# Folding the weights' halves before a merge, and ordering the transform's features by parity

## The chip, the cores and the metric

The kernel runs on one core of a Trainium2 chip. The metric is device time in microseconds (us) of one execution, the median of several runs. A core has TensorE (PE in the profile, its weight loads PEld), VectorE (DVE), ScalarE (ACT), GpSimd (POOL) and SyncE (SP, which issues most transfers). Each works through its own list in order and waits for the others by semaphores. SBUF is the working memory of 128 partitions, PSUM the eight banks into which TensorE adds.

## The reference

The input x has 8 batches of 3008 rows and 256 features. The reference takes a Fourier transform over the rows and one over the features, keeps the real part, and feeds the result to a gated layer:

```python
X = np.fft.fft(np.fft.fft(x, axis=1), axis=2).real
gate = 1.0 / (1.0 + np.exp(-(X @ w_gate)))      # w_gate, w_val: 256 x 1536
out = (gate * (X @ w_val)) @ w_out              # w_out: 1536 x 256
```

All is float32 in the result; the weights arrive as float64 and are turned to float32 on the chip.

## The kernel before

The transform over the rows is done with cosine and sine tables, on sums and differences of mirrored rows and features ("folds" of x). It leaves, per batch, two tiles of 128 features by 1505 frequencies: pk (cosine) and qk (sine). The transform over the 256 features is never done on the data. It is multiplied into the weights once: dt holds a 256 x 256 table (128 partitions, two halves t, 256 columns: 128 cosine and 128 sine), and a *merge* (`merge`, lines 410 to 421) multiplies it with a piece of 256 columns of w_gate or w_val. Out come pieces of G1 (for pk) and G2 (for qk). There are twelve such pieces, six for each of the two weights.

A piece goes through a chain on all engines. `weight_load` issues its transfer; `weight_parts` (ScalarE, lines 382 and 383) and `weight_join` (VectorE, lines 392 to 395, then GpSimd, line 397) turn float64 into float32; `weight_use` merges it: for each of two column halves h and each row half t of the weights one matmul, that is four calls in float32, and two copies by ScalarE (lines 417, 418) take the bank to G2 and G1. Two small transfers then put one row of G2 into ge. Float32 matmuls appear in the profile as two passes per call, so a merge counts 8 passes.

The order of work is written out by hand; there is no scheduler. After the start (lines 950 to 1015: the first two pieces, and batch 0's row transform) one loop runs over i, 576 times: 8 batches, 6 chunks of up to 252 frequencies, 12 blocks of 128 hidden columns. Per i, `front_a` and `front_b` multiply G1 with pk and G2 with qk into a bank (pf), `gate_a` and `gate_b` apply the gate on ScalarE and VectorE, with sums of blocks (sf) on GpSimd, and `back` multiplies with the output weights (po). Lists such as `use`, `join`, `pre`, `side`, `gap` and `mid` say at which i each further operation is put in; pieces 2 to 13 of the weights are merged at i = 0 to 8, alongside the first iterations.

Batch 0's row transform is done by `half` (line 595): banks ev and od, 24 matmul calls of 377 or 376 columns, from x folded by `half_rows` on VectorE. Batches 1 to 7 use `quarter` (line 620), twice per batch, put in by `mid`: 48 calls, each with 32 (or 31) partitions of x as weights and 95 columns of a table, four partition groups (TILES) writing four banks (sum). `e_sums` does a single feature (the 129th) with one or seven weight columns, placed in four column groups (pe).

In the first stage the order on VectorE is: joins of pieces 0 and 1, then the folds of x in four slices, then the join of piece 2 and the combining of ev and od into pk and qk. ScalarE has the copies of merges 0 and 1. On TensorE four calls named warm on dt come first, then merges 0 and 1, then pe, ev and od slice by slice.

Of the kernel before, what the change touches and what calls it, by code (L numbers as in the profile page):

```python
# [81 lines left out]
def kernel(  # L82
# [49 lines left out]
    def mm(o, l, r, start, stop):  # L132
        nc.tensor.matmul(o, l, r, start=start, stop=stop, skip_group_check=True)  # L133

    def bank(name, other=None):
        if other is not None:
            return pso.tile([P, 512], F32, name=name, tag=f"po{other}")
        return psx.tile([P, 512], F32, name=name, tag="x")
# [41 lines left out]
    wf = const.tile([P, NG, len(PLACE), P], F32, name="wf")  # L180
    G1 = const.tile([P, 2, F], F32, name="G1")
    G2 = const.tile([P, 2, F], F32, name="G2")
    ge = const.tile([P, 2, NFT], F32, name="ge")
# [99 lines left out]
    def quarter_ops():  # L283
# [28 lines left out]
        def ends_r():  # L312
# [10 lines left out]
            (0, 5), (1, 5), (2, 2), (2, 3), (2, 4), (2, 5)]  # L323
    RAW, WS = {}, {}
    shared = {}
    KEEP = 10

    def weight_load(j):
# [32 lines left out]
        else:  # L361
# [6 lines left out]
        raw = raw.bitcast(I32).rearrange("p (c f w) -> p c f w", c=2, w=2)  # L368
        ws = ws.rearrange("p (c f) -> p c f", c=2)
        WS[j] = ws  # L370
        if src.dtype == F32:
            nc.sync.dma_start(out=ws, in_=src)
        else:
            RAW[j] = raw
            nc.sync.dma_start(out=raw.rearrange("p c f w -> p c (f w)"), in_=src.bitcast(I32))  # L375
# [9 lines left out]
    def weight_join(j):  # L385
        if j not in RAW:
            return
        raw, ws = RAW.pop(j), WS[j]
        lo, hi = raw[:, :, :, 0], raw[:, :, :, 1]
        wi = ws.bitcast(I32)  # L390
        ts = nc.vector.tensor_scalar
        ts(out=ws, in0=ws, scalar1=2.0 ** -15, scalar2=HUGE, op0=ALU.max, op1=ALU.min)
        ts(out=wi, in0=wi, scalar1=3, scalar2=0x3FFFFFF8, op0=ALU.logical_shift_left,
           op1=ALU.bitwise_and)
        nc.vector.scalar_tensor_tensor(out=wi, in0=hi, scalar=-(2 ** 30), in1=wi,
                                       op0=ALU.bitwise_and, op1=ALU.bitwise_or)
        nc.gpsimd.tensor_tensor(wi, wi, lo, op=ALU.add)
# [5 lines left out]
    def weight_use(j):  # L403
# [3 lines left out]
        else:  # L407
            merge(WS.pop(j), w, c, (4, 2, 3)[next(turns) % 3] if j > 1 else None)

    def merge(ws, g, c, other):  # L410
        cs = slice(c * WC, (c + 1) * WC)
        ps = bank("ps", other)
        for h in range(2):
            for t in range(2):
                mm(ps[:, h * WC : (h + 1) * WC], dt[:, t, h * HD : (h + 1) * HD], ws[:, t, :],
                   h == 0 and t == 0, t == 1)
        nc.scalar.copy(G2[:, g, cs], ps[:, WC : 2 * WC])
        nc.scalar.copy(G1[:, g, cs], ps[:, 0:WC])
        for f in range(c * WC // P, (c + 1) * WC // P):
            nc.sync.dma_start(  # L420
                out=ge[:, g, f : f + 1], in_=G2[0:1, g, f * P : (f + 1) * P])

# [171 lines left out]

    def half(b, w, d, blk, sn, other=None):

# [23 lines left out]
    def quarter(b, blk):  # L620

        ps = [bank("sum", t + 1) for t in range(4)]
        for what in range(2):
            for part in range(2):
                for q in range(N3):
                    for t, (g, par, lo) in enumerate(TILES):
# [5 lines left out]
                        else:  # L632
                            w, tab = q + N3 * what, TAB["e4"][rows, what ^ g, q]
                        c0 = (2 * what + 1 - part) * NQ4
                        mm(ps[t][:, c0 : c0 + NQ4], W[b, blk][what][rows, w], tab,
                           what == part == q == 0, q == N3 - 1)
        for t, (g, par, lo) in enumerate(TILES):
# [335 lines left out]
    e0 = shared["qk"][:, 4 * WC : 4 * WC + CH]  # L973
    nc.gpsimd.memset(e0, 0.0)
    weight_parts(0)
    weight_parts(1)
# [26 lines left out]
    for f in places_c:  # L1003
        f()
    nc.scalar.copy(e0[0:1], E0[0][:, 0:CH])
    weight_parts(3)
# [239 lines left out]
```

## Time and profile before

| | |
|---|---|
| Median of 3 runs | 1908.67 us (1908.12 to 1909.44) |
| The profiled execution | 1909.15 us, of it span 1907.4 us |
| TensorE busy | 1895.6 us, 99% of the span, 11836 passes |
| VectorE, GpSimd, ScalarE busy | 1520.6, 1543.4, 1353.2 us |
| TensorE clock granted | 1.00 |
| Merges (ps) in the main loop | 10, each 8 passes, 1.73 us on the chain |
| Sum blocks (sum) | 14, each 96 passes, 2.86 us on the chain |

In the groups of the profile, a line such as "L133 PE MATMUL sum<-st,x x1344" names the line of the kernel, the engine, the operation, the tile written and those read, and the number of passes, then the least, median and greatest duration in ns. L133 is the line of the helper `mm`, so matmuls are told apart by their tiles. The duration of a matmul holds its way through the array; the distance of two starts says what one costs in a stream. In the timeline, brackets hold the idle time before an instruction and what ended it.

### The profile page before, as it was taken

Reading aid. Unit: us, or ns where it says so; the run is one execution under the profiler, and the core shown is the slowest. Engines: PE = TensorE matmul, PEld = TensorE weight load, DVE = VectorE, ACT = ScalarE, POOL = GpSimd, SP = SyncE. Lnnn points to the kernel's source line nnn. Section 1 sums busy time; section 2 is a strip of 40 time slices with the busy share of each in tenths; the row PEclk is TensorE's granted clock in tenths of the full one; section 3 lists DMA queues with packets and bytes.
Section 4 is the critical chain, followed back from the end, with each engine's and each line's share of the span. In section 5 each row is a group of like instructions: output and inputs, shape, how many; then the busy total and the mean of one; then the engine's idle time right before and its main releaser. Section 6 shows DMA issues by size and latency. Waiting matters only on the chain.

```text
span 1907.4 us, 36057 instructions
## 1 busy us (share of the span) xinstructions
PE 1895.6 (99%) x11836; PEld 1756.6 (92%) x11836; DVE 1520.6 (80%) x3375; ACT 1353.2 (71%) x3235; POOL 1543.4 (81%) x2733
## 2 busy tenths in 40 slices
PE   8999999999999999999999999999999999999999
PEld 5788999999999999999999999999999999999998
DVE  7678888878979778897788878888788777977775
ACT  4777777777777777777777777677767777777775
POOL 2489879987999779997799878999789986877770
PEclk9999999999999999999999999999999999999999
DMA  8446221212022121211211212122120110010001
GB/s 315 120 134 80 71 89 51 72 33 81 21 64 54 31 87 32 62 41 37 89 39 48 45 39 81 40 52 58 30 74 17 36 37 15 15 25 17 15 18 30
DMA packets 197333, 109.33 MB, mean 57 GB/s; under 512 B 134823, under 2 KB 188818, under 8 KB 195354
## 3 DMA queue, kind: packets, MB, share of 16 engines
q1 hardware_dynamic: 196568, 106.50, 21.1%
q8 instruction: 95, 1.56, 0.3%
q14 instruction: 92, 0.75, 0.1%
q10 hardware_dynamic: 546, 0.51, 0.1%
q0 software_dynamic: 32, 0.00, 0.0%
HBM read 71.24 MB, written 47.87 MB: 62 GB/s over the span
## 4 chain that ended last, share of the span: by engine, by line
PE 94%; DMA 2%; SPq 1%; POOL 1%; ACT 1%; DVE 0%; issue 0%; ACTq 0%; POOLq 0%
PE pf L133 49%; PE po L133 41%; PE sum L133 2%; DMA rtab<-in_stab_dram 1%; PE ps L133 1%; POOL sf L824 1%; DMA st<-in_stab_dram 1%; SPq L206 1%; DMA raw<-in_moe_w_val_dram 0%; PE od L133 0%; POOL x L507 0%; SPq L192 0%; SPq L375 0%; PE pe L133 0%; PE ev L133 0%
## 5 line engine op out<-in xcount | busy, mean ns | idle before, releaser
L824 POOL TENSOR_TENSOR sf<-h,sf 128x168 f32<-128x168 f32 (+1 forms) x1104 | 621.0, 582 | 79.5 <-DVE h L818 75.9
L824 POOL TENSOR_TENSOR sf<-h 128x168 f32<-128x168 f32 (+1 forms) x920 | 519.3, 584 | 159.8 <-DVE h L818 158.0
L133 PE MATMUL pf<-qk,G 128*128 128x252 f32 (+1 forms) x2304 | 583.4, 376 | 0.9 <-ACT ae L787 0.8
L133 PE MATMUL pf<-pk,G 128*128 128x252 f32 (+1 forms) x2304 | 582.7, 376 | 0.0
L772 ACT ACTIVATE pf<-ek,ge 128x252 f32<-128x252 f32 (+1 forms) x1142 | 538.2, 471 | 23.2 <-DMA ge<-G 3.0
L133 PE MATMUL po<-sf,wf 128*128 128x168 f32 (+1 forms) x2944 | 508.3, 305 | 0.0
L787 ACT ACTIVATE ae<-pf 128x504 f32<-128x504 f32 (+1 forms) x576 | 338.8, 588 | 218.7 <-PE pf L133 217.2
L133 PEld LDWEIGHTS pf<-pk,G 128*128 128x128 f32 x2304 | 435.9, 190 | 53.3 <-ACT pf L772 1.5
L133 PE MATMUL po<-h,wf 128*128 128x168 f32 (+2 forms) x2584 | 461.3, 307 | 0.0
L133 PEld LDWEIGHTS po<-sf,wf 128*128 128x128 f32 x2944 | 453.4, 190 | 8.0
L818 DVE TENSOR_TENSOR h<-pf,z 128x252 f32<-128x252 f32 (+1 forms) x576 | 240.4, 417 | 274.0 <-ACT pf L815 270.5
L802 DVE TENSOR_TENSOR z<-ae,pf 128x504 f32<-128x504 f32 (+1 forms) x576 | 384.6, 668 | 83.1 <-ACT h L801 79.1
L908 DVE TENSOR_TENSOR c<-c 128x168 f32<-128x168 f32 (+1 forms) x920 | 438.7, 500 | 3.3
L133 PEld LDWEIGHTS pf<-qk,G 128*128 128x128 f32 x2304 | 410.6, 190 | 32.3 <-ACT ae L787 2.1
L133 PEld LDWEIGHTS po<-h,wf 128*128 128x128 f32 x2584 | 410.4, 190 | 17.8 <-issue 0.9
L801 ACT ACTIVATE h<-pf 128x252 f32<-128x252 f32 (+1 forms) x576 | 216.9, 376 | 146.3 <-PE pf L133 129.0
L815 ACT ACTIVATE pf<-z 128x252 f32<-128x252 f32 (+1 forms) x576 | 214.3, 372 | 116.4 <-DVE h L814 114.5
L814 DVE TENSOR_TENSOR h<-h,pf 128x252 f32<-128x252 f32 (+1 forms) x576 | 232.9, 404 | 0.0
L824 POOL TENSOR_TENSOR sf<-sf 128x168 f32<-128x168 f32 (+1 forms) x184 | 101.7, 553 | 14.4
L824 POOL TENSOR_TENSOR sf<-sf,h 128x168 f32<-128x168 f32 (+1 forms) x184 | 110.1, 598 | 0.0
L891 ACT COPY c<-po 128x504 f32<-128x504 f32 (+1 forms) x138 | 78.5, 569 | 0.0
L918 DVE STREAM_TRANSPOSE os<-c 128x256 f32<-128x256 f32 x188 | 76.5, 427 | 0.1
(158 smaller groups left out, 876.4 us busy)
## 6 DMA issues: line engine op xcount, KB each, us to landing
x<-xr SPq DMA_DIRECT2D x14, 1536.0 KB
out_dram<-os SPq DMA_DIRECT2D x376, 56.0 KB
xr<-in_xf_dram SPq DMA_DIRECT2D x105, 128.0 KB
x<-x SPq DMA_DIRECT2D x112, 96.0 KB
xr<-in_xf_dram SPq DMA_DIRECT2D x14, 384.0 KB
ek<-ed SPq DMA_DIRECT2D x40, 126.0 KB
out_dram<-os SPq DMA_DIRECT2D x288, 7.0 KB
xr<-in_xf_dram SPq DMA_DIRECT2D x21, 124.0 KB
```

What stands on the lines that cost most here:

```text
L133: nc.tensor.matmul(o, l, r, start=start, stop=stop, skip_group_check=True)
L772: nc.scalar.activation(PF[i][:, g], EK[i // NFT], AF.Copy, scale=ge[:, g, f : f + 1])
L787: nc.scalar.activation(AP[i], PF[i], AF.Copy, scale=2.0)
L801: nc.scalar.activation(H[p][:, fh, 0:n], PF[i][:, 0], AF.Sigmoid)
L802: nc.vector.tensor_tensor(z[:, :, ::-1], AP.pop(i), PF[i], op=ALU.subtract)
L814: nc.vector.tensor_tensor(h[:, fh, 0:n], h[:, fh, 0:n], pf[:, 1], op=ALU.mult)
L815: nc.scalar.activation(pf[:, 0], z[:, 0], AF.Sigmoid)
L818: nc.vector.tensor_tensor(h[:, fh, n:], pf[:, 0], z[:, 1], op=ALU.mult)
L824: nc.gpsimd.tensor_tensor(block(p, dst), block(p, a), block(p, b), op=(ALU.subtract, ALU.add)[op])
L891: (nc.vector.tensor_copy if t == 1 or t == 3 else nc.scalar.copy)(C[0][:, 3 * t * R : 3 * (t + 1) * R], PO[t][:, 0 : 3 * R])
L908: nc.vector.tensor_tensor(t[:, dst * R : (dst + 1) * R], *v, op=(ALU.subtract, ALU.add)[op])
L918: nc.vector.transpose(os_[0][0][:, s, 0:nb, h, :], t[:, c0 : c0 + nb * TB])
```

## The change

Three things are changed together.

1. The table dt is reordered at the start by three VectorE copies: the odd cosines change places with the odd-numbered sines, so that every second column (e::2) of dt belongs to one parity of the feature. For pieces 2 to 13 of the gate and val weights, GpSimd makes the sum and the difference of the rows j and j + 128 after the join (two operations of 128 x 256). One parity of the features needs the sum alone, the other the difference alone, so a merge has two calls instead of four. Pieces 0 and 1 are not folded and keep four calls.
2. A merge's bank now holds features by parity, cosine in one half of the partitions and sine in the other. G1 and G2 become one tile G, and the bank is copied by partition halves: partitions 64 to 127 by VectorE (with the two halves exchanged), 0 to 63 by ScalarE, 64 x 512 each.
3. pk and qk must have their features in the same order. So each matmul of `half` and `quarter` becomes two (`mm2`), each with every second column of the weights, into one half of the bank's partitions: 64 columns instead of 128, and twice as many calls. The constant feature moves from partition 0 to partition 64 for qk, so ge and e0 take that row.

```diff
+    def mm2(o, l, r, start, stop, odd):
+        for e in range(2):
+            at_ = HP * (e ^ odd)
+            nc.tensor.matmul(o[at_ : at_ + HP], l[:, e::2], r, start=start, stop=stop, skip_group_check=True)
...
-    G1 = const.tile([P, 2, F], F32, name="G1")
-    G2 = const.tile([P, 2, F], F32, name="G2")
+    G = const.tile([P, 2, 2, F], F32, name="G")
+    G1, G2 = G[:, 0], G[:, 1]
...
+        if w < 2 and j > 1:
+            to = raw if j < KEEP else both[:, 10 + j % 2]
+            FOLD[j] = [to[:, i * WC : (i + 1) * WC] for i in range(2)]
...
     def weight_join(j):
-        if j not in RAW:
-            return
+        if j in RAW:
+            join_words(j)
+        for to, op in zip(FOLD.get(j, ()), (ALU.add, ALU.subtract)):
+            nc.gpsimd.tensor_tensor(to, WS[j][:, 0], WS[j][:, 1], op=op)
...
-            merge(WS.pop(j), w, c, (4, 2, 3)[next(turns) % 3] if j > 1 else None)
+            ws = WS.pop(j)
+            parts = [[x] for x in FOLD.pop(j)] if j in FOLD else [[ws[:, 0], ws[:, 1]]] * 2
+            merge(parts, w, c, (4, 2, 3)[next(turns) % 3] if j > 1 else None)
...
-        for h in range(2):
-            for t in range(2):
-                mm(ps[:, h * WC : (h + 1) * WC], dt[:, t, h * HD : (h + 1) * HD], ws[:, t, :],
-                   h == 0 and t == 0, t == 1)
-        nc.scalar.copy(G2[:, g, cs], ps[:, WC : 2 * WC])
-        nc.scalar.copy(G1[:, g, cs], ps[:, 0:WC])
+        for e, xs in enumerate(parts):
+            for t, x in enumerate(xs):
+                w = dt[:, t, e::2]
+                mm(ps[:, e * WC : (e + 1) * WC], w, x, e == 0 and t == 0, x is xs[-1])
+        ps = ps.rearrange("p (h n) -> p h n", h=2)
+        nc.vector.tensor_copy(G[HP:P, :, g, cs], ps[HP:P, ::-1])
+        nc.scalar.copy(G[0:HP, :, g, cs], ps[0:HP])
...
-    def half(b, w, d, blk, sn, other=None):
+    def half(b, w, d, blk, sn, other=None, mm=None):
+        mm = lambda *a: mm2(*a, int(sn))
...
-                        mm(ps[t][:, c0 : c0 + NQ4], W[b, blk][what][rows, w], tab,
-                           what == part == q == 0, q == N3 - 1)
+                        mm2(ps[t][:, c0 : c0 + NQ4], W[b, blk][what][rows, w], tab,
+                            what == part == q == 0, q == N3 - 1, what)
...
+    spare_ = evp.tile([P, NE], F32, name="a", tag="a")[:, 0:D].rearrange("p (c j) -> p c j", c=2)
+    cos_odd, sin_odd = dt[:, :, 1:HD:2], dt[:, :, HD + 1 :: 2]
+    for to, of in ((spare_[:, :, 0:HP], cos_odd), (cos_odd, sin_odd), (sin_odd, spare_[:, :, 0:HP])):
+        nc.vector.tensor_copy(to, of)
     weight_parts(0)
```

More of the change, by code (lines that the diff above doesn't have):

```diff
@@ L323 @@
             (0, 5), (1, 5), (2, 2), (2, 3), (2, 4), (2, 5)]
-    RAW, WS = {}, {}
+    RAW, WS, FOLD = {}, {}, {}
     shared = {}
@@ L367, in weight_load @@
                 ws = some(10, cp, "c")[:, i : i + 2 * WC]
-        raw = raw.bitcast(I32).rearrange("p (c f w) -> p c f w", c=2, w=2)
         ws = ws.rearrange("p (c f) -> p c f", c=2)
         WS[j] = ws
+        if w < 2 and j > 1:
+            to = raw if j < KEEP else both[:, 10 + j % 2]
+            FOLD[j] = [to[:, i * WC : (i + 1) * WC] for i in range(2)]
+        raw = raw.bitcast(I32).rearrange("p (c f w) -> p c f w", c=2, w=2)
         if src.dtype == F32:
@@ L385, in weight_join, with join_words @@
     def weight_join(j):
-        if j not in RAW:
-            return
+        if j in RAW:
+            join_words(j)
+        for to, op in zip(FOLD.get(j, ()), (ALU.add, ALU.subtract)):
+            nc.gpsimd.tensor_tensor(to, WS[j][:, 0], WS[j][:, 1], op=op)
+    def join_words(j):
         raw, ws = RAW.pop(j), WS[j]
@@ L407, in weight_use, with merge @@
         else:
-            merge(WS.pop(j), w, c, (4, 2, 3)[next(turns) % 3] if j > 1 else None)
-    def merge(ws, g, c, other):
+            ws = WS.pop(j)
+            parts = [[x] for x in FOLD.pop(j)] if j in FOLD else [[ws[:, 0], ws[:, 1]]] * 2
+            merge(parts, w, c, (4, 2, 3)[next(turns) % 3] if j > 1 else None)
+    def merge(parts, g, c, other):
         cs = slice(c * WC, (c + 1) * WC)
         ps = bank("ps", other)
-        for h in range(2):
-            for t in range(2):
-                mm(ps[:, h * WC : (h + 1) * WC], dt[:, t, h * HD : (h + 1) * HD], ws[:, t, :],
-                   h == 0 and t == 0, t == 1)
-        nc.scalar.copy(G2[:, g, cs], ps[:, WC : 2 * WC])
-        nc.scalar.copy(G1[:, g, cs], ps[:, 0:WC])
+        for e, xs in enumerate(parts):
[5 more added lines that the diff above has]
+        nc.scalar.copy(G[0:HP, :, g, cs], ps[0:HP])
         for f in range(c * WC // P, (c + 1) * WC // P):
             nc.sync.dma_start(
-                out=ge[:, g, f : f + 1], in_=G2[0:1, g, f * P : (f + 1) * P])
+                out=ge[:, g, f : f + 1], in_=G2[HP : HP + 1, g, f * P : (f + 1) * P])
     def forms(g):
@@ L1004 @@
         f()
-    nc.scalar.copy(e0[0:1], E0[0][:, 0:CH])
+    nc.scalar.copy(e0[HP : HP + 1], E0[0][:, 0:CH])
     weight_parts(3)
```

## The prediction

> **What bounds the kernel now.** I read the page's busy table and slices first, then the chain that ended last, then the groups of the tiles that the change touches, then the timeline of the first 60 us.
>
> ```profile
> PE 1895.6 (99%) x11836; PEld 1756.6 (92%) x11836; DVE 1520.6 (80%) x3375; ACT 1353.2 (71%) x3235; POOL 1543.4 (81%) x2733
> ...
> PE   8999999999999999999999999999999999999999
> ...
> PE 94%; DMA 2%; SPq 1%; POOL 1%; ACT 1%; DVE 0%; issue 0%; ACTq 0%; POOLq 0%
> PE pf L133 49%; PE po L133 41%; PE sum L133 2%; DMA rtab<-in_stab_dram 1%; PE ps L133 1%; POOL sf L824 1%; DMA st<-in_stab_dram 1%; SPq L206 1%; DMA raw<-in_moe_w_val_dram 0%; PE od L133 0%; POOL x L507 0%; SPq L192 0%; SPq L375 0%; PE pe L133 0%; PE ev L133 0%
> ```
>
> TensorE is the bound from about 33 us to the end, and the merges (ps) and the quarter sums (sum) are on the chain. A microsecond that TensorE saves or loses there moves the end, unless another engine takes over.
>
> Groups of the tiles sum, pe and ps, with two pieces of the chain (start, length, work):
>
> ```profile
> L133 PEld LDWEIGHTS sum<-st,x x1344: 181/187/187, 220.9 to 1610.4; 32*128 32x128 f32 x96, 31*128 31x128 f32 x96
> L133 PE MATMUL sum<-st,x x1344: 270/270/345, 220.9 to 1610.5; 32*128 32x95 f32 x96, 31*128 31x95 f32 x96
> ...
> L133 PEld LDWEIGHTS pe<-st,x x48: 79/86/100, 14.5 to 181.6; 128*1 128x1 f32 x24, 128*7 128x7 f32 x24
> L133 PE MATMUL pe<-st,x x48: 477/478/490, 14.5 to 182.0; 128*1 128x377 f32 x12, 128*1 128x376 f32 x12, 128*7 128x377 f32 x12, 128*7 128x376 f32 x12
> ...
> L133 PE MATMUL ps<-wx,dt x32: 379/379/380, 58.7 to 75.6; 128*128 128x256 f32 x32
> ```
> ```profile
> 64.02 1.73 PE ps L133 x8
> ...
> 180.35 2.09 PE pe L133 x23
> ...
> 220.99 2.86 PE sum L133 x96
> ```
>
> Every f32 matmul shows as two passes. A merge is 8 passes, 1.73 us. A sum block is 96 passes in 2.86 us, and there are 14 blocks (1344 / 96). In the single starts of a block, four passes, one for each quarter of rows, start within 20 ns, then nothing for 92 ns: one step each 111.5 ns, 24 steps.
>
> The start, from the timeline:
>
> ```profile
> 5.79 3.48 PE L133 MATMUL warm<-dt 128*128 128x256 f32 x8 [5.79 <-DMA dt<-in_dtab_dram]
> ...
> 10.18 1.22 DVE L494 TENSOR_TENSOR x<-x 128x1020 f32<-128x1020 f32 x1
> ...
> 10.38 2.15 POOL L397 TENSOR_TENSOR raw<-raw 128x512 int32<-128x512 int32 x1 [1.61 <-issue]
> ...
> 11.31 1.25 DVE L498 TENSOR_TENSOR x<-x 128x4 f32<-128x4 f32 x1
> ...
> 12.59 1.99 PE L133 MATMUL ps<-raw,dt 128*128 128x256 f32 x8 [1.58 <-POOL raw L397]
> ...
> 16.51 0.16 DVE L498 TENSOR_TENSOR x<-x 128x4 f32<-128x4 f32 x1
> ...
> 22.01 0.68 DVE L494 TENSOR_TENSOR x<-x 128x510 f32<-128x510 f32 x1
> ```
>
> VectorE folds x from 10.18 us without a pause until 24.6, and TensorE waits for each slice of it: this stage is VectorE's. A fold of four elements took 1.25 us beside GpSimd, 0.16 without it.
>
> **The change part by part.**
>
> *Quarter sums (14 blocks).* Each 32-row, 128-column matmul becomes two of 64 columns: 192 passes a block. What sets the 111.5 ns step? Streaming does not: a pf pass of 252 columns follows the next by 212.5 ns, 0.84 ns a column, so 95 columns need 80 ns. The weight load does: loads last 79 to 92 ns for 1 to 7 columns and 187 to 190 for 128, so 128 columns hold the load path about 108 ns. Do two halves run side by side? The nearest row is pe: four groups of columns, each with its own operands, pass 24 times 377 columns in 2.09 us, where one after another they need 24 x 0.316 = 7.6. So halves should run together, each load shorter by 64 x 0.85 = 54 ns, and the step falls to the 80 ns of streaming: 24 x 31.5 = 0.75 us less a block, 10.5 in all. At the other end the two loads of one row quarter follow each other: 2 x (108 - 54) + some 8 ns of two hand-overs = 116, +0.1 a block, +1.5. I take 0.5 us a block, two thirds of the gain, since eight tiles must be fed where four were and the block's first step (about 0.19 us) does not shrink: **-7.0 us**. The parity picks every second column of the weights; the strided weights of po<-h,wc load in 196 ns against 190, nothing. Copies out of the banks keep their shape.
>
> *First sequence sums (ev, od).* 48 pairs of passes, 377 columns each; by the pe row a pair costs what one cost, 0.316 us. 0, at most +0.3.
>
> *Merges.* Ten of twelve go from 8 passes to 4: 10 x 0.865 = 8.65 us less on TensorE between 37 and 76 us. What is late next? In an iteration such as the one from 46.80 to 51.08 us (4.28 us between two pf<-qk) TensorE would need 3.42. VectorE runs z at 0.68 to the second h at 0.41 in 2.86 us there, and now also copies half of each merge out of PSUM: the nearest row, a 128x504 copy on VectorE, is 0.67 us. That is 3.5 us, over 3.42, before GpSimd disturbs it. ScalarE loses two copies (0.36 and 0.38) for one of 0.57. GpSimd adds two folds of 128x256 after each join: by the 128x256 forms of L453, 0.73 us each, 1.46 per merge, 14.6 in all, in a window (36 to 80 us) where it is busy 14.4 of 44 us. Throughput is there; latency is not always: joins ended 0.7 to 0.9 us ahead of the merge for the merges that start at 63.86 and 68.98, so these folds end about 0.6 late. And a VectorE op that meets GpSimd waits: L393 took 1.41 us at 38.12 and 61.61 beside a join, 0.43 alone; twice the GpSimd work means more such meetings, about 0.5 to 0.9 us each. Ends: the full -8.65, and +2 if every fold is waited for. I take half of the full gain, since three of the merges sit where ScalarE set the pace (pf<-qk at 40.69 waits for ae) and three where VectorE is full: **-4.3 us**.
>
> The Trainium skill (GPSIMD Engine Reference, 1. Specifications) says that GpSimd shares its SBUF interfaces with VectorE, against ops in a two-port mode or with two SBUF inputs. The trace agrees for L393; h (L814, one input in PSUM) stays at 0.41. By the rule alone the folds x of the first stage would meet it too, and the merges would bring nearer 2 than 4 us.
>
> *The start.* Three VectorE copies on dt (128x128 each, about 0.2 us by the four-element fold's 0.16 and 0.42 for 254 elements) stand ahead of the first join: +0.6, and warm waits for them. More: the VectorE half of the copies of merges 0 and 1 now stands in VectorE's order ahead of the folds of x. Before, ScalarE held both. So the folds wait for merge 1: join about 10.5, GpSimd 1.3 (without VectorE beside it, not 2.15), merge 1.99, copy 0.67: they begin near 14.5 instead of 10.18. The fold that lost 1.1 us beside GpSimd no longer does. Everything behind, TensorE's sums and the first pf at 33.05, moves by 4.4 - 1.1: **+3.3 us**, between +2 (a quicker join) and +5. SP's order is unchanged; its transfers are issued ahead of need or follow the loop, so the 0.76 us wait for tables at 147.8 us moves with it.
>
> *Sum.* -7.0 - 4.3 + 3.3 = -8.0. The profiled execution took 1909.15 us, 1907.4 of it span; 1901.1 in its terms, and 0.5 less against the median of 1908.67: 1900.7.
>
> **The rivals.**
> - *Loads one after another.* The halves of a row quarter share a load path (no row shows two wide loads of one row group): sums +1.5, sum +0.5: 1909. For it: only narrow loads ran side by side in pe. Against: nothing shown.
> - *Halves one after another.* If the two column halves of 32-row tiles do not stream together, the step is 2 x 81: 24 x 50.5 = +1.2 a block, +17, total 1925 with the other terms. It decides as soon as a step exceeds 111.5 + 2.9 ns, where the +1 rest of the other two terms (-4.3 + 3.3) is used up. Against: pe.
> - *A rate per pass.* Passes come at 29.8 ns on average in a block (2.86 / 96). If that is the issue rate, 192 take 5.72: +40, 1948. Against: four passes start within 20 ns, and four calls of pe passed within 0.07 us after a wait.
>  The Trainium skill (TensorE: Matmul & The Clock Gate, Wait — 56ns, not 53.3ns?) gives a floor of about 25 ns between matmul starts, however short. By it a block of 192 takes 4.8 us, an estimate, and the kernel ends near 1935; the starts 6 to 7 ns apart on different row quarters speak against it across tiles.
> - *Folds late.* Sums as forecast, merges +3 by waits for GpSimd and VectorE: 1908.
>
> **How the numbers follow.** Forecast 0.57, loads in turn 0.17, halves in turn 0.12, rate 0.08, folds late 0.06. Alone the forecast spans 1892 to 1907 (sums -10.5 to -3, merges -8.65 to 0, start +2 to +5, not all at one end). The range 1892 to 1925 leaves out the rate, part of the halves and a low tail, under 0.2. A measurement here tells 0.2%, 3.8 us, from nothing. Faster: 0.47 of the forecast and 0.03 of the loads: 0.50. Same: 0.25, mostly loads and late folds. Slower: 0.25, the halves, the rate and tails.
>
> **What would show it.** A sum block on the chain near 2.3 to 2.4 us with 192 passes says that the halves run together; 2.9 to 3.0 loads in turn; 4.1 halves in turn; over 4.8 a rate. The ps pieces halve to 0.87 us; if the first po then starts less than 3 us earlier relative to the first pf, VectorE or GpSimd took the rest, and ps or pf shows waits for G or for POOL. The first pf should come near 36.3 us, with VectorE idle ahead of its first G copies. Wrong sums are what would make the forecast wrong most.

## The result and the profile after

The changed kernel takes 1935.96 us, median of 4 runs (1935.39 to 1936.17), against 1908.74 us (1908.12 to 1909.44) for the kernel before in the same comparison. The ratio is 1.0141, with a 95% interval of 1.0125 to 1.0157: slower by 27 us, where 8 us faster had been forecast. The profiled execution took 1935.92 us, of it span 1933.8, so 26.4 us more than the span before.

The busy table, two of the slice rows and the chain of the page, as shown for the kernel before:

```profile
PE 1896.9 (98%) x13188; PEld 1747.8 (90%) x13188; DVE 1531.8 (79%) x3390; ACT 1353.2 (70%) x3223; POOL 1558.9 (81%) x2753
...
PE   6899999999999999999999999999999999999999
...
PEclk8999999999999999999999999999999999999999
...
PE 91%; DMA 2%; DVE 2%; SPq 1%; POOL 1%; ACT 1%; issue 1%; ACTq 0%; POOLq 0%
```

TensorE's busy time is about what it was, and its share of the chain fell from 94 to 91%: 25 of the 26 us are time in which it stood (36.9 us without a pass in the span, 11.8 before). The first two slices (48 us each) hold 15.6 of these 25; most of the rest lies behind "issue 1%", where the engine waited for nothing that the profile names. The waits of TensorE, longest in total first (time in total, times, longest), split it further:

```profile
PE sum L139 <- issue: 8.4, 8, 1.8
PE warm L133 <- DVE dt L995: 6.3, 1, 6.3
PE pf L133 <- ACT ae L804: 5.8, 5, 3.6
PE ev L139 <- DVE x L597: 3.0, 2, 1.5
PE pe L133 <- DVE x L523: 2.9, 1, 2.9
PE ev L139 <- DMA x<-in_xf_dram: 2.5, 1, 2.5
```

The second row is harmless (before, warm waited 5.8 us for the table itself). From single starts the loss can be laid out by place. Here and below, a step is a group of four pf passes, counted from 0, so the pf of step 32 is the 129th pf pass; the time from the first pf to it, in which the weights are merged, is called the stretch.

| | before | after | difference |
|---|---|---|---|
| first pf at | 33.05 us | 45.69 us | +12.6 |
| from there to the pf of step 32 | 59.99 us | 64.74 us | +4.8 |
| the 14 sum blocks, each from the pf pass before it to the twelfth pf pass behind it | | | +9.3 |
| everything else | | | -0.3 |

Three places, then, and each is one that the prediction had a step for.

*The start*, from the timeline (start, length, engine and line, in brackets the idle time before and its cause):

```profile
11.93 0.69 DVE L433 COPY G<-ps 64x512 f32<-64x512 f32 x1 [1.70 <-PE ps L133]
...
13.74 0.69 DVE L433 COPY G<-ps 64x512 f32<-64x512 f32 x1 [1.11 <-PE ps L133]
...
14.48 1.22 DVE L510 TENSOR_TENSOR x<-x 128x1020 f32<-128x1020 f32 x1
...
21.25 1.53 PE L139 MATMUL ev<-st,x 128*64 128x377 f32 x4 [2.54 <-DMA x<-in_xf_dram]
...
24.07 1.22 DVE L510 TENSOR_TENSOR x<-x 128x1020 f32<-128x1020 f32 x1 [5.39 <-PE od L139]
...
31.27 0.69 DVE L510 TENSOR_TENSOR x<-x 128x510 f32<-128x510 f32 x1 [1.58 <-PE od L139]
```

The first three rows are as forecast: VectorE copies both merges, and the folds of x begin at 14.48 us. The last three are not. The fold of the second slice of x waits 5.39 us for a sum of the first slice, though it reads and writes other bytes; the first ev, whose x was folded by 18.7 us, waits until 21.25 for a transfer of x. Folds and sums take turns, where before they ran side by side.

*The sum blocks.* First a block that went well and then one that did not, in pieces of the chain (start, length, work):

```profile
279.04 2.59 PE sum L139 x142
```
```profile
431.87 2.42 PE sum L139 x130
434.29 1.65 issue
435.94 0.41 PE sum L139 x11
436.35 2.62 PE po L133 x10
438.97 2.39 PE pf L133 x8
```

The good one has 2.59 us where 2.86 stood before: the halves do run side by side. From the pass before the block to the pass behind, a clean block takes 2.87 us against 3.17. In eight of the 14 TensorE stands once inside the block, and in a ninth just behind it, 0.5 to 2.1 us each, 11.7 us in all; behind the stand shown here the next passes also run at half speed (eight pf passes in 2.39 us, where they take 1.70; the granted clock from 436 to 440 us is 0.60). Counting TensorE's instructions (each pass is a weight load and a matmul, so a block has 384 where it had 192) shows one thing in common: every one of these stands is at an instruction whose number, counted from the first record of the trace, leaves 193 when divided by 256. Below, a stretch of 256 instructions is called an instruction page, and the instruction with that number its end. The profile's row of instruction transfers fits that, before and after:

```profile
q8 instruction: 95, 1.56, 0.3%
```
```profile
q8 instruction: 105, 1.72, 0.4%
```

(packets, MB, share). TensorE's passes go from 11836 to 13188, 1352 more, which are 2704 instructions, 10.6 times 256; ten more packets of 0.0164 MB came.

### The profile page after: what moved, and what is told of

Its sections match the earlier page's. It is cut to its first block, busy times and chain, and to the rows that moved or that the text cites. A ratio compares the mean times of both kernels' runs of the same rounds, so it can differ in the third digit from the quotient of the medians.

```text
span 1933.8 us, 38795 instructions
## 1 busy us (share of the span) xinstructions
PE 1896.9 (98%) x13188; PEld 1747.8 (90%) x13188; DVE 1531.8 (79%) x3390; ACT 1353.2 (70%) x3223; POOL 1558.9 (81%) x2753
## 4 chain that ended last, share of the span: by engine, by line
PE 91%; DMA 2%; DVE 2%; SPq 1%; POOL 1%; ACT 1%; issue 1%; ACTq 0%; POOLq 0%
PE pf L133 48%; PE po L133 40%; PE sum L139 2%; DMA rtab<-in_stab_dram 1%; POOL sf L841 1%; DMA x<-in_xf_dram 1%; SPq L212 1%; PE od L139 0%; PE ev L139 0%; DMA raw<-in_moe_w_val_dram 0%; SPq L253 0%; DVE z L819 0%; ACT ae L804 0%; DMA st<-in_stab_dram 0%; PE ps L133 0%
```

## The experiments

Theory A, formed from these two traces: (1) overlap of strided regions is judged by their outer bounds, so the stride of the half weights makes folds and sums wait for each other; (2) VectorE's copies of G delay the folds at the start and ScalarE behind it; (3) TensorE's instructions come in pages of 256, and two page ends too close in time make it stand. Rivals: 64-column products or strided reads are slow in themselves; GpSimd's folds hold the early loop; what runs beside a block makes it stand. Where the features of weights and sums do not match, the expectation says so.

### The sums whole again

```diff
-                        mm2(ps[t][:, c0 : c0 + NQ4], W[b, blk][what][rows, w], tab,
-                            what == part == q == 0, q == N3 - 1, what)
+                        mm(ps[t][:, c0 : c0 + NQ4], W[b, blk][what][rows, w], tab,
+                           what == part == q == 0, q == N3 - 1)
```

> The changed kernel with one edit: each call of the quarter sums is one 128-column product again (features in their old order, so the output's features are mixed up; no work is left out). In the changed kernel the 14 blocks take 52.2 us from the pass before to the pass behind, in the old kernel 44.35. Theory (the halves run side by side, but eight of the blocks stand 0.5 to 2.1 us once, always at the 193rd instruction of a page of 256 on TensorE, so twice the instructions is what costs): the blocks are back at 44.4 us, time 1928 us (1927 to 1929). Rival (the forecast's gain of 7 us is there and the loss lies elsewhere): 1943 us.

Measured: 1926.18 us against 1908.43, ratio 1.0095 (1.008 to 1.011), a little below the 1927 to 1929 expected. By the table's measure the 14 blocks are at +0.0, each within 0.01 us of the kernel before. The time falls by 9.8 us instead of 7.9: the expectation had counted the blocks up to the pass behind, and the passes at half speed come after that.

### Sums split in the kernel before, and their place in the stream

The next run splits only the quarter sums of the kernel before (`mm2` with `l[:, at_ : at_ + HP]`, neighbouring columns, so the features keep their order):

```diff
-                        mm(ps[t][:, c0 : c0 + NQ4], W[b, blk][what][rows, w], tab,
-                           what == part == q == 0, q == N3 - 1)
+                        mm2(ps[t][:, c0 : c0 + NQ4], W[b, blk][what][rows, w], tab,
+                            what == part == q == 0, q == N3 - 1)
```

> The kernel before with one edit: each call of the quarter sums split in two halves of 64 neighbouring columns (all else as before). Theory of the instruction pages: a page of 256 instructions ends at index 193 modulo 256; counted on from the kernel before, the blocks of 384 hold a page's end at position 320, 258, 392, 330, 275, 213, 414, 352, 297, 235, 180, 374, 319, 257, so nine of the 14 (the 1st, 2nd, 4th, 5th, 8th, 9th, 12th, 13th, 14th) stall by 0.5 to 2.1 us, and the 3rd, 6th, 7th, 10th, 11th run in 2.9 us (3rd perhaps 0.1 to 1.4 more just behind it); sum of the stalls 12.5 us, of the gains 14 x 0.30 = 4.2, time 1917 us (1914 to 1919). Rival (the halves are merely slower or faster alike in all blocks): each block 2.87 us and 1904.5 us, or all blocks alike longer.

Measured: 1917.64 us against 1908.43, ratio 1.0054 (1.0039 to 1.0069). Of the nine blocks named, seven stood (0.8 to 2.8 us), two (page ends at 258 and 257) did not; the third stood 1.3 us just behind; all others ran clean. Then the same kernel with small products in front, which move everything behind them in TensorE's stream and change nothing else:

```diff
+    for i in range(64):
+        mm(warm[0:1, 0:1], nil[:, 0, 0:1], nil[:, 0, 0:1], True, True)
     for i in range(4):
         mm(warm[:, 0:WC], dt[:, 0, 0:P], dt[:, 0], True, True)
```

> The kernel before with the quarter sums split in contiguous halves (1917.6 us) and one more edit: 64 one-element products at the very start, while TensorE has nothing to do, so that all that follows stands 128 instructions later in its stream. Theory of the pages: the page ends in the 14 blocks move to positions 192, 386, 264, 202, 403, 341, 286, 224, 425, 363, 308, 246, 191, 385; so the 1st, 4th, 8th, 13th (2.8 + 1.8 + 1.9 + 1.8 us of standing before) run in 2.8 to 2.9 us and the 6th, 7th, 10th, 11th (clean before) stand 0.8 to 2 us; time 1912 to 1918. Rival (standing hangs on what runs beside each block, transfers or other engines): the same blocks stand as before.

Measured: 1920.95 us, ratio 1.0059 (1.0042 to 1.0076), and the same blocks stood at the same positions. The expectation had miscounted: a float32 product is two passes, four instructions, so 64 of them are 256, one whole page. By the theory nothing was to move, and nothing did; the rival says the same, so the run does not tell them apart. With `range(32)`, half a page:

> The kernel before with the quarter sums split in contiguous halves (1917.6 us), and 32 one-element products at the very start: each is four of TensorE's instructions, so all that follows stands 128 later, half a page (the 64 of the run before this were a whole page, and every block stood where it had stood). Theory of the pages: the page ends in the 14 blocks move to positions 192, 386, 264, 202, 403, 341, 286, 224, 425, 363, 308, 246, 191, 385; the 1st, 4th, 8th, 13th (2.8 + 1.8 + 1.9 + 1.8 us of standing) run clean and the 6th, 7th, 10th, 11th (clean so far) stand by 0.8 to 2 us; time 1913 to 1919. Rival (what runs beside a block decides): the 1st, 4th, 5th, 8th, 9th, 12th, 13th stand as they did.

Measured: 1915.28 us against 1908.84, ratio 1.0032 (1.0019 to 1.0044). All eight blocks that were named did as expected, the seventh with a stand of only 0.4 us. The position of the instruction page's end in each block of 384 and the time that TensorE stood there, in us ("-" below 0.2):

| block | changed kernel | split | split, half a page later |
|---|---|---|---|
| 1 | 291: 0.8 | 320: 2.8 | 192: - |
| 2 | 229: - | 258: - | 386: 1.5 |
| 3 | 363: 1.9 | 392: 1.3 | 264: 0.8 |
| 4 | 301: 1.6 | 330: 1.8 | 202: - |
| 5 | 246: 0.9 | 275: 0.8 | 403: 0.8 |
| 6 | 184: - | 213: - | 341: 1.5 |
| 7 | 385: 1.4 | 414: - | 286: 0.4 |
| 8 | 323: 2.1 | 352: 1.9 | 224: - |
| 9 | 268: 0.5 | 297: 1.0 | 425: - |
| 10 | 206: - | 235: - | 363: 1.9 |
| 11 | 407: - | 180: - | 308: 1.9 |
| 12 | 345: 1.7 | 374: 1.6 | 246: - |
| 13 | 290: 0.9 | 319: 1.8 | 191: - |
| 14 | 228: - | 257: - | 385: 1.7 |

The sixth block in pieces of the chain, split and then half a page later:

```profile
687.85 1.49 PE pf L133 x7
689.33 2.53 PE sum L138 x141
691.87 1.62 PE po L133 x10
```
```profile
687.40 2.26 PE sum L138 x126
689.67 1.29 issue
690.96 0.55 PE sum L138 x19
691.51 1.62 PE po L133 x10
```

The same block, the same work beside it, and it stands or not by its place in the stream: what runs beside it is out. In these columns no block stood with its page ends at 180 to 235 or from 407 on; with an end at 264 to 392 all 23 did. Over all the traces with split blocks there are a few exceptions: of 71 ends at 264 to 392, two (282 and 283) cost only 0.1 us, and a block with its end at 228 stood 0.7 us. In the blocks of the table that stood with the end before 50 instructions or more inside them, the two ends came 3.1 to 3.7 us apart (once 4.5), stand included; 256 instructions of a clean split block take about 1.6 us, and around the blocks of the kernel before no two page ends came closer than 8.5 us.

The traces also hold every transfer of q8 by itself, 16384 bytes each, and this tells what is waited for. In each of the 17 traces there are as many of them as TensorE has page ends (95 to 106; in one trace one more), so each page end can be paired with a transfer. In the blocks just named the transfer of the first end began 0.7 to 1.4 us behind it and lasted 0.9 to 1.7 us, and TensorE crossed the next end 1.3 to 1.5 us after that. In all 17 traces no page end was crossed sooner than 1.2 us after the end of the transfer paired with the page end before it, and where TensorE's next start there came more than 0.6 us after the last, 74 times in or just behind the blocks, it was 1.2 to 1.6 us after it. So TensorE waits for its own instructions: the next page is there some 3 us after the last one's end, and the split sums ask for it sooner. The Trainium skill (Trainium Architecture — The Big Picture, The software stack) has instructions of 64 bytes. By that figure a page is 16 KB, an estimate, and the size of a q8 transfer here agrees.

### The first sums whole again

```diff
     def half(b, w, d, blk, sn, other=None, mm=None):
-        mm = lambda *a: mm2(*a, int(sn))
+        mm = lambda *a: mm1(*a)
```

`mm1` is the product of 128 columns.

> The changed kernel with one edit: the first sequence's sums (ev, od) are 128-column products of a contiguous weight tile again (features in their old order, so the output is not the reference's; no work is left out). Theory (the strided weight tile of each half makes folds of x wait for sums that read other bytes, and the first sum wait for later loads of x, which turns a side-by-side start into turns): those waits go, the first pf comes near 37.3 us (33.05 of before plus the 4.3 by which the folds begin later) in place of 45.69, time 1927.5 us (1926 to 1930). Rival (the start is late through VectorE's copies of G and of the table, and TensorE at half clock only follows from that): first pf stays above 43 us, time 1934 to 1936.

Measured: 1932.23 us (1928.97 to 1934.95), ratio 1.0125 (1.0109 to 1.014). The first pf came at 38.08 us, near the 37.3 expected; the time fell only by 3.7 and missed its range, because 24 calls fewer ahead of the blocks put them elsewhere in the pages: by the table's measure the blocks are at +13.7 us instead of +9.3. From here on stretches are compared, not only times. How far chance goes there is seen in the runs that split only the quarter sums: the first pf came at 32.6 to 33.9 us in their profiles, and the stretch took 59.8 to 60.2.

### The first sums split in the kernel before

By parity (`l[:, e::2]`, as in the changed kernel), and then by neighbouring columns (`l[:, at_ : at_ + HP]`); nothing else differs.

```diff
-                mm((ev, od)[q % 2], w(q), ST[int(sn)][0:NP, q, c0 : c0 + n], q < 2, q >= NQ - 2)
+                mm2((ev, od)[q % 2], w(q), ST[int(sn)][0:NP, q, c0 : c0 + n], q < 2, q >= NQ - 2)
```

> The kernel before with one edit: the first sequence's sums split in two 64-column halves by parity, as in the changed kernel (the output's features are permuted; nothing is left out, weights are not folded, merges stay as they were). Theory of the waits: the folds and sums take turns here too, first pf at 33.05 + 8.4 = about 41 us, time about 1917 us (1914 to 1919). Rival (the turns only arise because the folds begin late in the changed kernel): 1909 us, first pf at 33 to 34.

> The kernel before with one edit: the first sequence's sums split in two halves of 64 neighbouring columns (contiguous weight tiles; output as the reference). The same split by parity (strided tiles) took 1919.7 us with its first pf at 44.44 us, the kernel before 33.05. Theory (it is the stride, through waits on bytes that do not overlap, that costs 11 us): the waits are gone, first pf 33 to 34 us, time 1908 to 1910. Rival (64-column products or twice the calls cost it by themselves): first pf above 40 us, time 1916 to 1920.

Measured: by parity 1919.74 us, ratio 1.0058 (1.0042 to 1.0075), first pf at 44.44; by neighbouring columns 1909.2 us, ratio 1.0000 (0.999 to 1.0009), first pf at 33.01. Twice the calls in halves of 64 cost nothing; the stride costs 11 us, more than the 8.4 expected. Its timeline:

```profile
21.54 1.52 PE L138 MATMUL ev<-st,x 128*64 128x377 f32 x4 [6.21 <-DMA x<-in_xf_dram]
```
```profile
24.36 1.22 DVE L499 TENSOR_TENSOR x<-x 128x1020 f32<-128x1020 f32 x1 [8.88 <-PE od L138]
```

The folds begin at 10.19 us here, as before the change, and then that of the second slice waits 8.88 us for od.

### The stride kept, x laid out by row

```diff
-        X[b] = xp.tile([P, 4, NQ, D], F32, name="x4", tag="x4")
+        X[b] = xp.tile([P, 4, NQ, D] if b else [P, NQ, 4, D], F32, name="x4", tag="x4")
+        if not b:
+            X[b] = X[b].rearrange("p q h d -> p h q d")
...
-        nc.sync.dma_start(out=X[0][0:NP, :, q : q + n], in_=xf[0, :, :, q : q + n])
+        for q in range(q, q + n):
+            nc.sync.dma_start(out=X[0][0:NP, :, q], in_=xf[0, :, :, q])
```

> The changed kernel with one edit: x of the first sequence lies in SBUF by row (row, part, feature) in place of (part, row, feature), and the two double loads are four single ones, so that what one fold and one sum touch is one stretch of bytes that no other row's stretch overlaps. All arithmetic, the strided halves too, is as in the changed kernel. Theory (the waits between sums and folds of other rows come from overlap judged by the outer bounds of strided regions): they go, first pf 37 to 39 us as in the run with contiguous first sums, and with the changed kernel's own page positions the time is 1935.96 - 7.6 = 1928 us (1926 to 1930). Rival (64-column strided reads of the weights are slow in themselves): first pf above 43, 1934 to 1936.

Measured: 1929.61 us against 1908.84, ratio 1.0109 (1.0094 to 1.0124), first pf at 38.37. In its timeline the second slice's fold follows the first without a wait, and ev waits only for its own fold:

```profile
18.18 1.41 DVE L600 TENSOR_TENSOR x<-x 128x508 f32<-128x508 f32 x2
19.52 1.21 DVE L513 TENSOR_TENSOR x<-x 128x1020 f32<-128x1020 f32 x1
```
```profile
19.64 1.52 PE L139 MATMUL ev<-st,x 128*64 128x377 f32 x4 [0.64 <-DVE x L602]
```

The strided reads are all still there, so they are not slow in themselves. With neighbouring columns the old layout had no such waits, and by row the stride has none: it takes both, a strided read and a layout in which a row's four parts span the other rows. That overlap is judged by the outer bounds of a region, as theory (1) has it, fits both runs but is not shown by itself; and the single loads in place of double ones, part of this edit, may have a share in the wait of ev for its load. 7.3 of the 12.6 us at the start are these waits.

### The copies of G by ScalarE

Both runs below copy both halves by ScalarE; the first starts from the kernel with whole first sums, the second from the one with x by row.

```diff
-        nc.vector.tensor_copy(G[HP:P, :, g, cs], ps[HP:P, ::-1])
+        nc.scalar.copy(G[HP:P, :, g, cs], ps[HP:P, ::-1])
```

> The changed kernel with contiguous first sums (1932.2 us; first pf 38.08, pf of step 32 at 102.47, so 64.4 us between them, against 60.0 in the kernel before) and one more edit: both copies of a merge's bank to G by ScalarE, none by VectorE (output features permuted as in that run). Theory of the copies (VectorE's 0.69 us copy comes late in VectorE's queue, ScalarE's copy of the other half and with it the release of pf stand behind it, 18.5 us in ten waits): the 64.4 us become 57 to 59 us, time 1925 to 1928. Rival (GpSimd's folds of the pieces, 8.0 us of waits, or ScalarE's own load set it): 63 to 66 us, time unchanged within 1.5 us.

> The changed kernel with x of the first sequence by row, and with both copies of a merge to G by ScalarE. Theory (waits of the overlap 7.6 us, VectorE's copies 5.1 at the start and 2.9 in the 32 steps behind, pages 7.9): first pf 33 us, 61.5 us from there to step 32, time 1935.96 - 7.6 - 5.1 - 2.9 = 1920 us (1918 to 1923); what is left over the kernel before is the pages' 7.9 and 2 to 3 us of ScalarE's copies of 64 partitions. Rival (the three causes overlap, so that two of them removed together give less than their sum): 1924 to 1928.

Measured: 1923.23 us against 1909.07 (1.0074, 1.0059 to 1.0089) and 1920.72 against 1908.84 (1.0061, 1.0046 to 1.0076). In both the first pf moves by 5.1 us, to 32.99 and 33.30, and the stretch behind it by 2.8, from 64.4 to 61.5 us. The first run had expected 57 to 59 us there and its rival 63 to 66, so VectorE's copies are only a part of what the stretch loses. The second run met its sum of three separate causes within a microsecond. The tile ps with VectorE's copies (who copies, times and ns; then what ended the idle time of those who work on ps: us, times), and with ScalarE's:

```profile
L435 DVE COPY G<-ps x12: 689/695/696, 13.0 to 86.0; 64x512 f32<-64x512 f32 x12
L436 ACT COPY G<-ps x12: 570/579/582, 13.7 to 86.7; 64x512 f32<-64x512 f32 x12
...
  DVE G L435: 18.5, 10
```
```profile
L435 ACT COPY G<-ps x12: 581/582/585, 11.9 to 78.0; 64x512 f32<-64x512 f32 x12
L436 ACT COPY G<-ps x12: 579/580/581, 12.5 to 78.6; 64x512 f32<-64x512 f32 x12
```

and in the kernel before:

```profile
L417 ACT COPY G<-ps x12: 344/358/372, 11.0 to 76.4; 128x256 f32<-128x256 f32 x12
L418 ACT COPY G<-ps x12: 359/378/384, 11.3 to 76.6; 128x256 f32<-128x256 f32 x12
```

With VectorE's copies ScalarE waited 18.5 us, in ten merges, for the copy of the other half; why the one copy has to wait for the other was not tested. And the shape costs by itself: 64 partitions by 512 take 0.58 us where 128 by 256 take 0.37, so a bank's two copies take 1.16 us of one engine instead of 0.74. Between the first pf and step 32 ScalarE is then busy 52.7 of 62 us, where it was 47.5 of 61 (sums of five windows, the first run above and the kernel before):

```profile
sum 62.00, PE 54.78 PEld 38.50 DVE 46.50 ACT 52.72 POOL 38.25; mean PE 10.96 PEld 7.70 DVE 9.30 ACT 10.54 POOL 7.65
```
```profile
sum 61.00, PE 61.00 PEld 47.23 DVE 42.66 ACT 47.53 POOL 23.80; mean PE 12.20 PEld 9.45 DVE 8.53 ACT 9.51 POOL 4.76
```

### No folds by GpSimd

```diff
-        if w < 2 and j > 1:
+        if False:
             to = raw if j < KEEP else both[:, 10 + j % 2]
```

> The changed kernel with contiguous first sums and one more edit: no piece is folded by GpSimd, each merge takes its eight instructions as before, in the changed order of features; the copies stay one by VectorE and one by ScalarE (output features permuted). Theory of the copies: the stretch of 64.4 us from first pf to step 32 stays or grows, 64 to 69 us, since TensorE gets 8.65 us of work back that partly fills its waits; time 1932 to 1937. Rival (the folds on GpSimd cost the stretch): it falls to 60 to 62 us, time 1928 to 1930.

Measured: 1932.33 us against 1909.07, ratio 1.0123 (1.0108 to 1.0138). The stretch takes 63.46 us, between the two expectations: with VectorE's copies in place the fold is worth nothing, it costs 0.9 us, little more than chance. The first pf comes at 36.98 us instead of 38.08, so the fold may cost something ahead of it too. The copies stay the larger part.

### The fold alone

GpSimd's folds in the kernel before, with nothing else of the change: for each column half h of the table two products of 64 columns, one per parity, into the two partition halves, so that the copies keep their 128 x 256.

```diff
-        for h in range(2):
-            for t in range(2):
-                mm(ps[:, h * WC : (h + 1) * WC], dt[:, t, h * HD : (h + 1) * HD], ws[:, t, :],
-                   h == 0 and t == 0, t == 1)
+        for h in range(2):
+            for t in range(len(parts[0])):
+                for e, xs in enumerate(parts):
+                    mm(ps[e * HP : (e + 1) * HP, h * WC : (h + 1) * WC], dt[:, t, h * HD + e : (h + 1) * HD : 2],
+                       xs[t], h == 0 and t == 0, t == len(xs) - 1)
```

> The kernel before with the folding of the weight pieces alone: GpSimd's two folds per piece, each merge two pairs of 64-column halves side by side, copies by ScalarE as before; x and the sums stay in their old order, so the features of weights and sums do not match and the output is not the reference's (no work is left out). Forecast's step: the merges give 4.3 us (of 8.65 that TensorE saves), stretch from first pf to step 32 55.7 us, time 1904.4. Theory after the runs so far (the pieces come through ScalarE, VectorE and GpSimd no faster than every 4 to 5 us, so TensorE only waits instead of working): stretch 59 to 60 us, time 1908 to 1909.5.

Measured: 1908.42 us against 1909.22, ratio 0.9996 (0.9987 to 1.0005), stretch 59.50 us where 55.7 had been forecast and 59.99 stood before. The folded merges start at 41.42, 45.36, 49.12, 52.89, 57.63, 62.92, 69.02 and 74.49 us, where the last before were 41.65, 45.07, 49.35, 53.63, 58.74, 63.86, 68.98 and 74.09: TensorE has less to do for each, but the last one is no earlier. All its waits between 33 and 95 us:

```profile
PE pf L133 <- ACT ae L797: 1.0, 1, 1.0
PE ps L133 <- POOL wx L392: 1.0, 3, 0.4
PE pf L133 <- ACT G L428: 0.8, 1, 0.8
```

These waits count only idle time; from start to start the loss is larger. Three of the ten merges wait for a late fold in between and take 1.70 to 2.09 us, where an undisturbed one takes 1.02. And the gain of an undisturbed merge is less than counted: 1.02 us against 1.73, with 0.09 more on the way in and 0.10 behind, so about 0.52 us instead of 0.865, since passes of 64 columns next to passes of 128 start 306 to 317 ns apart where 213 to 216 is usual. The Trainium skill (TensorEngine Tiling (Array Packing), Key Properties) says that a change of tiling mode drains TensorE. The longer distances at these changes agree with that.

### Features by parity from the folds of x

To have the output right without split sums, the folds of x themselves write the features by parity (in GpSimd's folds by two more small copies each); merges as in the run above, x of batch 0 by row.

```diff
-            e.tensor_tensor(r[:, q, 1:HD], v[:, q, 1:HD], v[:, q, D - 1 : HD : -1],
-                            op=ALU.subtract)
-            e.tensor_tensor(v[:, q, 1:HD], v[:, q, 1:HD], v[:, q, D - 1 : HD : -1], op=ALU.add)
+            up = v[:, q, D - 1 : HD : -1]
+            for o in (0, 1):
+                at_ = slice(o * HP + 1 - o, o * HP + HP)
+                e.tensor_tensor(r[:, q, at_], v[:, q, 2 - o : HD : 2], v[:, q, D - 2 + o : HD : -2], op=ALU.subtract)
+            e.tensor_tensor(up, v[:, q, 1:HD], up, op=ALU.add)
+            for o in (0, 1):
+                at_ = slice(o * HP + 1 - o, o * HP + HP)
+                e.tensor_copy(v[:, q, at_], v[:, q, D - 2 + o : HD : -2])
```

> The kernel before with the folding alone in another layout: the folds of x write the features by parity (even features in the lower half), so all sequence sums stay 128 contiguous columns and no more instructions; a merge of a folded piece is two pairs of 64-column halves side by side whose results stand as whole 128-partition tiles, copied by ScalarE in two copies of 128x256 as before; x of the first sequence by row. Output as the reference. GpSimd does the folds of the weights and two more small copies per fold of x (about 0.9 us each, 42 of them); VectorE gets three more small instructions per slice of the first folds. Theory (what the folding saves on TensorE, 8.65 us between the first pf and step 32, was lost to the copies' shape and the sums' doubling): first pf 33 to 35 us, the stretch 54 to 58 us in place of 60.0, blocks of sums 44.3 us in all, time 1903 to 1907. Rival (GpSimd, which folds late, or ScalarE holds the stretch): stretch 60 to 62, time 1909 to 1912.

Measured: 1925.65 us against 1908.84, ratio 1.0088 (1.0073 to 1.0103), above both expectations. First pf 33.52, stretch 59.42 and the blocks as before the change; what was expected of the stretch was wrong, as the run above then showed by itself. The time went at two other places, 4.8 us near 165 and 8.5 near 355. The chain there:

```profile
351.21 3.48 POOL sf L845 x7
...
356.52 0.54 POOL x L522 x2
...
357.08 0.48 DVE x L584
357.57 0.34 DVE h L839
...
357.93 0.48 ACT pf L793
```

GpSimd was already busy 29.5 of the 30 us from 330 in the kernel before; its new copies (L522) come late, VectorE's next step on x (L584) stands 9.3 us for them, where it stood 1.7 before, and the gate's work queued behind it on VectorE, then ScalarE and TensorE wait along.

### All three causes out of the changed kernel

x by row, copies by ScalarE, sums as whole products; left are the folds, the parity and its copies of 64 partitions, the table's copies and the split first sums.

```diff
-                        mm2(ps[t][:, c0 : c0 + NQ4], W[b, blk][what][rows, w], tab,
-                            what == part == q == 0, q == N3 - 1, what)
+                        mm(ps[t][:, c0 : c0 + NQ4], W[b, blk][what][rows, w], tab,
+                           what == part == q == 0, q == N3 - 1)
```

> The changed kernel with x of the first sequence by row, both copies of G by ScalarE, and the quarter sums as 128-column products (output features mixed, no work left out). What is left of the change is the folded merges with copies of 64 partitions, the table's three copies and the first sums in two strided halves. Theory (three separate causes): first pf 33.3 us, the stretch behind it 61.5, blocks 44.3 us, time 1910 to 1911.5, the 1.5 to 2.5 us over the kernel before being the stretch. Rival (the folded merges or the split first sums cost more, in a place not seen yet): 1913 or more.

Measured: 1912.06 us against 1909.22, ratio 1.0015 (1.0006 to 1.0024); first pf 33.29, stretch 61.11, blocks at +0.0. Each against the kernel before of its own comparison, the excess goes from 27.2 us (changed) to 20.8 (x by row), 11.9 (copies by ScalarE too) and 2.8 (sums whole too): 6.4 us are the waits', 8.9 the copies', 9.0 the sums', taken out in this order, and 2.8 are what the fold with its copies of 64 partitions still loses. That is a little more than expected. The profiled execution, the fastest of the ten, has a span 1.5 us longer than the kernel before; 0.2 of that lie ahead of the first pf and 1.1 in the stretch behind it.

### Only the blocks that the pages allow

```diff
     def quarter(b, blk):
+        call = mm2 if next(COUNT) in (1, 3, 4, 6, 7, 9, 12) else mm
...
-                        mm(ps[t][:, c0 : c0 + NQ4], W[b, blk][what][rows, w], tab,
+                        call(ps[t][:, c0 : c0 + NQ4], W[b, blk][what][rows, w], tab,
```

> The kernel before with only seven of the 14 blocks of quarter sums split in contiguous halves: the 2nd, 4th, 5th, 7th, 8th, 10th and 13th, chosen by counting instructions so that no page ends between positions 241 and 397 of a split block (page ends at 194, 202, 147 and 403, 222, 160 and 416, 235, 191). Output as the reference. Theory of the pages: each of the seven takes 2.82 to 2.88 us in place of 3.17, none stands (the 5th, with a page's end 19 instructions behind its last, perhaps 0.7 just behind it), the other seven stay at 3.17; time 1906.0 to 1907.5, so 1.2 to 2.3 us below the kernel before. Rival (split blocks stand for another reason about as often as not): 1912 us or more.

Measured: 1906.9 us (11 runs, 1906.59 to 1907.89) against 1909.22 (27 runs), ratio 0.9988 (0.9979 to 0.9997). None of the seven blocks stood inside; two were followed by a gap of 0.4 and 0.2 us (ends at 403 and 416). The fourth block on the chain:

```profile
452.21 1.70 PE pf L133 x8
453.91 2.53 PE sum L138 x135
456.44 1.62 PE po L133 x10
```

It is the one version of these whose whole interval lies below the kernel before, by 0.12%.

## Why the prediction was wrong, step by step

- **Quarter sums, -7.0.** That the halves run side by side was right, and with it the three rivals on the sums (loads in turn, halves in turn, a rate per pass) fall. By the Trainium skill (TensorE: Matmul & The Clock Gate, Wait — 56ns, not 53.3ns?) starts are never closer than about 25 ns. Here 192 passes of four row quarters and two column halves take 2.4 us, 12.5 ns each, so for passes on different tiles the trace does not agree. The size was off: a clean block gains 0.30 us, not 0.5, so 4.2 in all. What failed is that the step counted the doubled passes only as a rate, not as instructions that have to be brought: the stands at page ends cost 11.7 us, the slower passes behind one of them 1.7, and -7.0 became +9.3.
- **First sequence sums, 0, at most +0.3.** True of the arithmetic: split by neighbouring columns they cost nothing (1.0000). The step looked at passes and not at what a strided weight does to the waits of VectorE and TensorE on each other. That cost 7.3 us here and 11.4 in the kernel before alone.
- **Merges, -4.3.** Measured -0.5, no more than chance, when made alone and with cheap copies, and +4.8 as the change has them. The working was about throughput: it found VectorE at 3.5 us against 3.42 for TensorE and still took half. Three sizes were wrong. ScalarE's copy waits for VectorE's, which comes late in a full queue (18.5 us in ten merges). Two copies of 64 x 512 take ScalarE 1.16 us where two of 128 x 256 take 0.74. And what TensorE saves turns into waiting even without those copies: with the fold alone it waits for late folds by GpSimd and for ScalarE.
- **The start, +3.3.** The mechanism was right, and without VectorE's copies, and without the waits of the first sums, the first pf is back at 33.0 us. The size was 5.1, at the upper bound of its range: the 1.1 us subtracted for the fold beside GpSimd was gained (L514 took 0.16 us), but the folds begin at 15.4 to 15.5 us in the runs that show this step alone, 0.9 us later than forecast, and TensorE ran its first passes behind the wait at about half its clock (granted 0.57 from 19.6 to 23 us with x by row).
- **The sum and the range.** The first pf was forecast near 36.3 us and came at 45.69. The rival that named late folds gave the merges +3, by waits for GpSimd and VectorE, and had the sign; VectorE's copies were the larger part. None of the rivals had the waits of the start or the instruction pages. No single step puts the time outside the range, whose upper end is 24.3 us above the forecast: the sums are 16.3 us off, the merges 9.1, the first sums 7.3 and the start 1.8, together 34.5. That 1935 us, worked out in the prediction from a floor per pass, is close to the time is chance: by it every block would take 4.8 us, and the clean ones take 2.6.

## What to carry to other kernels

Before doubling the number of calls in a burst, count instructions: in these runs a burst of 384 short TensorE instructions stood in 69 of 71 cases in which an instruction page ended at its 264th to 392nd, and the same work with the ends elsewhere was mostly a gain. A strided view in place of a contiguous one can change which waits are made, so compare the waits of the two programs engine by engine, and lay out a tile so that what is used apart lies apart. And a layout that puts results on half of the partitions doubles what every copy behind it has to do per partition (0.58 us against 0.37 here); work saved on the bound engine is worth only what the slowest chain feeding it lets through.

## What the runs showed of the hardware that was not expected

- TensorE stands for its own instructions: in bursts of about 6 ns per instruction mostly 3.1 to 3.7 us from one page end of 256 instructions to the end of the next stand (up to 5.4 in two runs, where the transfer began late), and never less than 1.2 us from the end of the 16 KB transfer to the page end behind it.
- Starts of passes on different row quarters and column halves came 12.5 ns apart on average and often 6 to 7 ns, with steps of eight passes between 81 and 136 ns.
- After some waits TensorE runs at about half its clock for a while. At the start of the changed kernel passes of 377 columns started 628 ns apart instead of 316, and behind the stand of the third block passes of 252 columns 418 ns apart instead of 213; behind the longer stand of the eighth block they did not (granted clock 1.00 from 943 to 947 us). Windows of the changed kernel (length, busy time and count by engine, then the granted clock, the DMA's share and GB/s):

```profile
21.00:28.00 7.00, 6.75 (x24) 2.86 (x24) 2.68 (x4) 0.00 (x0) 0.00 (x0) 0.56 1.06 380
28.00:34.00 6.00, 3.05 (x20) 1.16 (x20) 3.86 (x10) 0.00 (x0) 0.00 (x0) 1.00 1.05 386
```

  The kernel before has 1.00 in both. A late start thus costs more than its wait; how much of the 12.6 us is the clock was not measured by itself.
